# Three of four late modulation rows: from matrix-vector products on TensorE to sums on VectorE and DMA transposes

## The chip, the core and the metric

The kernel runs on one core of one Trainium2 chip. The metric is the device time of one launch in microseconds (us), the median of ten runs. The engines of a core have names used throughout: PE is TensorE (matrix products; PEld its weight loads), DVE is VectorE, ACT is ScalarE, POOL is GpSimd, and SP is the engine that here only issues DMA transfers. Each runs its own instructions in the order in which the program lists them, and waits on semaphores for the others.

## What is computed

In short form below: a transformer block with adaptive LayerNorm: a linear-attention part A and a gated feed-forward part B, both modulated by six vectors that come from a condition `c` of 1024 numbers. Sequence length S is 2048, width D 1024, feed-forward width F 3584, 32 heads of 32; inputs and output are bfloat16.

```python
mod = (silu(c) @ w_mod).reshape(c.shape[0], 6, 1, -1)
sa, ca, ga, sb, cb, gb = (mod[:, i] for i in range(6))
h = layernorm(x) * (1 + ca) + sa
q, k, v = split(h @ wqkv)
num, den = phi(q) @ (phi(k).T @ v), phi(q) @ sum(phi(k))
x = x + ga * ((num / (den + 1e-6)) @ wo)
h = layernorm(x) * (1 + cb) + sb
x = x + gb * ((silu(h @ w_gate) * (h @ w_up)) @ w_down)
```

The six vectors are six rows of 1024 numbers: each is `silu(c)` (1024) times a 1024 x 1024 block of `w_mod`. `sa` and `ca` are needed first of all. The other four, `ga`, `sb`, `cb` and `gb`, are the "late" rows. `sb` and `cb` are applied to activations whose features lie on the partitions, so they are wanted as a [128, 8] tile (feature 128 c + p at partition p, column c). `ga` and `gb` scale columns, so they are wanted spread to all 128 partitions, as the [128, 1024] tiles `ga_bc` and `gb_bc`.

## The kernel before

The 2048 positions are handled in four chunks (`sc` 0 to 3) of four tiles of 128. Groups of work on TensorE have labels, and a list written out by hand gives their order:

- V, Q and K groups: ("K", sc, i), ("V", sc, i) with i from 0 to 7, and ("Q", sc, qc). A group is eight matrix products into one PSUM bank. The order is V of chunk 0, then Q of chunk 0, K and V of chunk 1, K and V of chunk 2, K and V of chunk 3, then Q of chunks 1, 2 and 3. ("KV", sc, 0) and ("KV", sc, 1), 16 small products each into banks 5 to 7, stand before and after the first group that follows chunk sc. The text calls a label K2,3 for short, and V2 the stage of eight V groups of chunk 2.
- ("GU", sc, f) with f from 0 to 27: one gate and one up product of the feed-forward part; ("D", st, h): the down products.

`put(label, ...)` hangs further work behind a group: it is issued, on whatever engine, after that group's own instructions, and in the order in which it was put. Since every engine is in order, a label is a place in the queue of each engine that the work uses, SP's DMA queue among them.

Around the change there is this work. `phi_to` (lines 235 to 239) empties each K and Q bank: an exponential on ACT, two instructions on DVE; V banks are emptied by ACT alone. Groups take their banks in turn from five. `ln` (line 216) does the LayerNorm of one tile of the next chunk: statistics on DVE, then a power, a product and the normalisation on POOL (lines 202 to 211), then a DMA transpose on SP (line 220). It hangs behind K1,1, K1,3, K1,5 and K1,7, and the same in K2. `modulate` (line 222, two halves behind V1,4 and V1,6, and in V2) applies `sa` and `ca` on DVE to the transposed tiles, and the K groups of the next chunk read the result, one of eight slices per product. `kvz_build` (line 278) makes `KVZ` behind KV3,1; `nd_mm` (line 428) multiplies by it from Q1,3 on and normalises on DVE; `o_mm` (line 455) multiplies by `wo`.

The late rows before the change: `load_late` (line 290) brings half a row, a 1 MB block [128, 8, 512], in one of three slots `wml`; eight of them are issued from V0,6 to K2,6. `late_mm` (line 295), behind K1,2, K1,6, V1,2, V1,6, K2,2, K2,6, V2,2 and V2,6, does 32 matrix-vector products (weights 128x128, one column of `scT`) for half a row; DVE copies the finished row from PSUM to `m1`. `late_fin` makes `sbT` and `cb1T` from it, or for `ga` and `gb` a copy `rep` that repeats each column 128 times. `late_bc` (line 314, behind V1,1 and K3,1) multiplies `rep` by the identity into two banks, and ACT copies them to `ga_bc` or `gb_bc`. `wo` is loaded behind K2,0, and each of its eight slices is multiplied by `ga_bc` on DVE behind V3,0 to V3,7 (line 602). `warm` (line 185) issues products with zeros at the start.

The memory is laid out by hand: `view` cuts tiles from big regions (`M3`, `M5` and others), and tiles that live at different times share addresses.

Of the kernel before, what the change touches and what calls it, by code (L numbers as in the profile page):

```python
# [9 lines left out]
ALU = mybir.AluOpType  # L10
BF16 = mybir.dt.bfloat16
F32 = mybir.dt.float32
# [9 lines left out]
def kernel(  # L22
# [13 lines left out]
    nc = tc.nc  # L36
    P = nc.NUM_PARTITIONS
    _, S, D = A_x.shape
# [3 lines left out]
    DC = D // P  # L42
# [5 lines left out]
    NB = 512  # L48
    NH = D // NB
# [13 lines left out]
    wo_v = A_wo.rearrange("(c p) n -> p c n", p=P)  # L63
# [3 lines left out]
    wm_v = w_mod.rearrange("(p j) n -> p j n", j=DC)  # L67
    c_v = c.rearrange("o (p j) -> p (o j)", j=DC)

    const = ctx.enter_context(tc.tile_pool(name="const", bufs=1))  # L70
    dram = ctx.enter_context(tc.tile_pool(name="dram", bufs=1, space=DRAM))
    psum = ctx.enter_context(tc.tile_pool(name="psum", bufs=1, space=PSUM))
    small = ctx.enter_context(tc.tile_pool(name="small", bufs=6))
    epool = ctx.enter_context(tc.tile_pool(name="epool", bufs=4))

    x1_dram = dram.tile([S, D], F32, name="x1_scratch")
    bank = [psum.tile([P, NB], F32, name=f"bank{i}") for i in range(8)]

# [8 lines left out]
    def view(region, off, shape, dtype=BF16):  # L87
        n = 1
        for s_ in shape:
            n *= s_  # L90
        w = n * (2 if dtype == F32 else 1)
        ap = region[:, off:off + w]
        if dtype == F32:
            ap = ap.bitcast(F32)
        if len(shape) == 2:
            ap = ap.rearrange("p (a b) -> p a b", a=shape[0])
        elif len(shape) == 3:
            ap = ap.rearrange("p (a b c) -> p a b c", a=shape[0], b=shape[1])
        return ap
# [8 lines left out]
    wml = [view(M3, 4096 * (1 + i), [DC, NB]) for i in range(3)]  # L108
# [9 lines left out]
    wo = view(M6, 0, [DC, D])  # L118
    x1rs = [view(M6, 2048 * i, [D], F32) for i in range(2)]
    obs = [view(M6, 4096 + 1024 * i, [D]) for i in range(2)]  # L120
    yts = [view(M6, 6144 + 1024 * i, [NB], F32) for i in range(2)]
    xs = [view(M7, 1024 * i, [D]) for i in range(6)]
    xns = [view(M7, 6144 + 1024 * i, [D]) for i in range(6)]
    wgs = [view(M7, 4096 * i, [DC, FBW]) for i in range(3)]
# [11 lines left out]
    def load_x(st):  # L136
        nc.sync.dma_start(out=xs[st % 6], in_=x2[st * P:(st + 1) * P, :])
# [22 lines left out]
    load_wk(6, 7)  # L160
    load_wk(7, 8)

    zt = const.tile([P, NB], BF16, name="zt")
    nc.vector.memset(zt[:], 0.0)
# [15 lines left out]
    rep = const.tile([P, DC, P], BF16, name="rep")  # L180

    scT = const.tile([P, DC], BF16, name="scT")
    nc.scalar.activation(out=scT[:], in_=c_sb[:], func=ACT.Silu)

    def warm(n):
        for _ in range(n):
            nc.tensor.matmul(bank[7][:], lhsT=zt[:, 0:P], rhs=zt[:], start=True, stop=True)


    stat = {}  # L190
# [39 lines left out]
    def nextbank():  # L230
        b = bank[state["b"]]
        state["b"] = (state["b"] + 1) % 5
        return b
# [51 lines left out]
                                    in1=mask[:, P:KVW].unsqueeze(1).to_broadcast([P, n, HPC]), op=ALU.mult)  # L285


    LATE = [(2, "ga"), (3, "sb"), (4, "cb"), (5, "gb")]

    def load_late(i):  # L290
        q, kb = LATE[i // 2][0], i % 2
        k0 = q * D + kb * NB
        nc.sync.dma_start(out=wml[i % 3], in_=wm_v[:, :, k0:k0 + NB])

    def late_mm(i):
        q, kb = LATE[i // 2][0], i % 2
        mps = bank[7][:, 320 + 8 * q:328 + 8 * q]
        for ii in range(NB // P):
            col = kb * (NB // P) + ii
            for j in range(DC):  # L300
                nc.tensor.matmul(mps[:, col:col + 1], lhsT=wml[i % 3][:, j, ii * P:(ii + 1) * P],  # L301
                                 rhs=scT[:, j:j + 1], start=False, stop=(j == DC - 1), skip_group_check=True)
        if kb == 1:
            nc.vector.tensor_copy(out=m1[:, q, :], in_=mps[:, 0:DC])

    def late_fin(q):
        if q == 3:
            nc.vector.tensor_copy(out=sbT[:], in_=m1[:, 3, :])
        elif q == 4:
            nc.vector.tensor_scalar_add(out=cb1T[:], in0=m1[:, 4, :], scalar1=1.0)  # L310
        else:
            nc.vector.tensor_copy(out=rep[:], in_=m1[:, q, :].unsqueeze(2).to_broadcast([P, DC, P]))

    def late_bc(q, dst):
        for h in range(NH):
            b = nextbank()
            for i in range(NB // P):
                cc = h * (NB // P) + i
                nc.tensor.matmul(b[:, i * P:(i + 1) * P], lhsT=rep[:, cc, :], rhs=ident[:], start=True, stop=True)
            nc.scalar.copy(out=dst[:, h * NB:(h + 1) * NB], in_=b[:])  # L320


    def tr0(st):
# [40 lines left out]
    ln_xn(0, False)  # L364
    tr0(0)
    warm(3)
    ln_xn(1, False)
    tr0(1)
# [56 lines left out]
    def put(label, *fns):  # L425
        after.setdefault(label, []).extend(fns)
# [157 lines left out]
    put(("V", 0, 6), lambda: load_late(0), lambda: load_late(1), lambda: load_late(2))  # L584
# [12 lines left out]
    put(("K", 2, 0), lambda: nc.sync.dma_start(out=wo, in_=wo_v))  # L597
    put(("K", 2, 7), lambda: late_fin(4))
    put(("V", 2, 7), lambda: late_fin(5))
    put(("K", 3, 1), lambda: late_bc(5, gb_bc))  # L600
    for cc in range(DC):
        put(("V", 3, cc), lambda cc=cc: nc.vector.tensor_tensor(out=wo[:, cc, :], in0=wo[:, cc, :], in1=ga_bc[:],
                                                               op=ALU.mult))


    put(("KV", 3, 1), kvz_build)
# [77 lines left out]
```

## Time and profile before

| | us |
|---|---|
| median of ten runs | 847.27 |
| lowest, highest | 847.04, 849.18 |
| the profiled execution, its own time | 847.66 |
| its span, first to last instruction | 845.9 |

The profile is of one execution. Its times are counted from the span's start; what lies around the span is 847.66 - 845.9 = 1.8 us. Its granted TensorE clock was 1.00. A line of a timeline has the start, the length (both us), the engine, the line of the source, the instruction, output<-input with shapes, the count of instructions merged in it, and in brackets how long the engine had been idle and what ended that. A row of a group table ends with total busy us, mean ns of one, and the idle time before. A row of DMA issues ends with the median us from issue to landing.

The stages lie like this in the span (us):

| stage | from | to |
|---|---|---|
| K1 | 61.1 | 76.5 |
| V1 | 76.5 | 93.6 |
| K2, with both KV1 | 93.6 | 110.8 |
| V2 | 110.8 | 126.2 |
| K3, with both KV2 | 126.2 | 142.3 |
| V3 | 142.3 | 156.1 |
| Q1 to Q3, with `nd_mm` and `o_mm` | 156.1 | 216.4 |
| GU of chunk 0 | 216.4 | 327 |

### The profile page before, as it was taken

To read this page: it belongs to the slowest core of one execution; us is meant where nothing else is said; L and a number is where in the kernel's file an instruction comes from. 1 tells how busy PE (TensorE), PEld (TensorE's weight loads), DVE (VectorE), ACT (ScalarE), POOL (GpSimd) and SP (SyncE) were. 2 spreads that over 40 slices of the span, in tenths; PEclk is the share of its full clock that TensorE was granted. 3 is DMA by queue.
4 is the path that set the end of the run, shared out by engine and by line. 5 is a ranking of instruction groups with operands and counts; after the bars stand their busy time and mean duration, and the time that the engine had idled before them with its cause. 6 is when DMAs were issued, how large, how long until landed. Compare 5 with 4: busy or idle time off the path is not lost.

```text
span 845.9 us, 10977 instructions
## 1 busy us (share of the span) xinstructions
PE 837.5 (99%) x4452; PEld 395.5 (47%) x4452; DVE 322.9 (38%) x617; ACT 144.8 (17%) x270; POOL 78.9 (9%) x142
## 2 busy tenths in 40 slices
PE   8999999999999999999999999999999999999998
PEld 4454554544444444444444444444444444444444
DVE  5667456488755655421111222211122122112222
ACT  4333223322211111111110001111000111100000
POOL 2124130013122323100000000000000000000000
PEclk9999999999999999999999999999999999999999
DMA  9995982056489988878876215555322555201220
GB/s 292 305 239 133 276 196 54 1 126 159 96 222 216 216 215 212 195 230 255 245 232 178 69 60 163 150 150 149 106 75 70 152 156 156 84 19 62 76 69 26
DMA packets 203763, 128.65 MB, mean 152 GB/s; under 512 B 50496, under 2 KB 189888, under 8 KB 203712
## 3 DMA queue, kind: packets, MB, share of 16 engines
q1 hardware_dynamic: 162864, 98.58, 41.0%
q10 hardware_dynamic: 38544, 20.98, 11.7%
q0 software_dynamic: 2304, 8.39, 2.6%
q8 instruction: 35, 0.57, 0.3%
q14 instruction: 16, 0.13, 0.1%
HBM read 103.81 MB, written 12.58 MB: 138 GB/s over the span
## 4 chain that ended last, share of the span: by engine, by line
PE 96%; DVE 1%; SPq 1%; DMA 1%; issue 0%; ACT 0%; DVEq 0%
PE bank L530 23%; PE bank L511 23%; PE bank L505 23%; PE bank L462 7%; PE bank L265 7%; PE bank L257 6%; PE bank L242 5%; DMA M<-in_w_mod_dram 1%; PE bank L435 1%; PE bank L274 1%; PE bank L301 1%; SPq L145 1%; SPq L142 0%; DVE stats L196 0%; DVE M L239 0%; DVE e L238 0%
## 5 line engine op out<-in xcount | busy, mean ns | idle before, releaser
L511 PE MATMUL bank<-M,M 128*128 128x512 bf16 x896 | 211.7, 379 | 0.0
L505 PE MATMUL bank<-M,M 128*128 128x512 bf16 x896 | 211.6, 379 | 0.0
L513 DVE TENSOR_TENSOR M<-bank,e 128x512 bf16<-128x512 f32 x112 | 77.5, 692 | 275.1 <-PE bank L511 274.0
L530 PE MATMUL bank<-M,M 128*128 128x512 bf16 (+1 forms) x700 | 147.9, 370 | 0.0
L508 ACT ACTIVATE e<-bank 128x512 f32<-128x512 f32 x112 | 66.8, 597 | 439.7 <-PE bank L505 433.4
L530 PEld LDWEIGHTS <-M 128*128 128x128 bf16 x924 | 90.4, 98 | 103.3
L511 PEld LDWEIGHTS <-M 128*128 128x128 bf16 x896 | 87.7, 98 | 105.7
L505 PEld LDWEIGHTS <-M 128*128 128x128 bf16 x896 | 87.3, 98 | 103.9
L534 DVE TENSOR_TENSOR M<-bank,gb_bc 128x512 f32<-128x512 f32 (+1 forms) x33 | 22.3, 676 | 149.2 <-PE bank L530 149.2
L242 PE MATMUL bank<-M,M 128*128 128x512 bf16 x256 | 58.2, 379 | 1.0 <-DVE M L224 0.6
L462 PE MATMUL bank<-M,M 128*128 128x512 bf16 x256 | 57.9, 379 | 0.0
L265 PE MATMUL bank<-M,M 128*128 128x512 bf16 x256 | 57.5, 379 | 0.0
L257 PE MATMUL bank<-M,M 128*128 128x512 bf16 x256 | 56.7, 379 | 0.0
L237 ACT ACTIVATE e<-bank 128x512 f32<-128x512 f32 x64 | 37.8, 598 | 101.9 <-PE bank L265 48.4
L530 PE MATMUL bank<-M 128*128 128x512 bf16 x224 | 51.0, 379 | 0.0
L239 DVE SCALAR_TENSOR_TENSOR M<-bank,e 128x512 bf16<-128x512 f32 x64 | 44.3, 691 | 3.7
L238 DVE TENSOR_SCALAR e<-e 128x512 f32<-128x512 f32 x64 | 27.7, 433 | 40.6 <-ACT e L237 40.5
L462 PEld LDWEIGHTS <-M 128*128 128x128 bf16 x256 | 24.9, 98 | 29.8
L257 PEld LDWEIGHTS <-M 128*128 128x128 bf16 x256 | 24.7, 98 | 29.1
L265 PEld LDWEIGHTS <-M 128*128 128x128 bf16 x256 | 24.6, 98 | 27.9
L242 PEld LDWEIGHTS <-M 128*128 128x128 bf16 x256 | 24.0, 97 | 28.8 <-DVE M L224 2.1
L464 DVE TENSOR_TENSOR M<-bank,M 128x512 f32<-128x512 f32 x32 | 22.1, 690 | 14.5 <-PE bank L462 14.3
(66 smaller groups left out, 333.9 us busy)
## 6 DMA issues: line engine op xcount, KB each, us to landing
M<-in_B_w_gate_dram SPq DMA_DIRECT2D x56, 512.0 KB, 3.9
M<-in_B_w_up_dram SPq DMA_DIRECT2D x56, 512.0 KB, 5.1
M<-in_w_mod_dram SPq DMA_DIRECT2D x8, 1024.0 KB, 7.4
x_scratch<-M POOLq DMA_DIRECT2D x16, 512.0 KB, 5.7
M<-x_scratch ACTq DMA_DIRECT2D x16, 512.0 KB, 3.5
M<-in_B_w_down_dram SPq DMA_DIRECT2D x6, 1024.0 KB, 8.0
M<-in_A_x_dram SPq DMA_DIRECT2D x16, 256.0 KB, 6.7
M<-in_w_mod_dram SPq DMA_DIRECT2D x8, 512.0 KB, 8.2
```

The costliest lines, as they stand in the source:

```text
L237: nc.scalar.activation(out=e[:], in_=acc, func=ACT.Exp)
L238: nc.vector.tensor_scalar(out=e[:], in0=e[:], scalar1=1.0, scalar2=PHI_EPS, op0=ALU.min, op1=ALU.add)
L239: nc.vector.scalar_tensor_tensor(out=dst, in0=acc, scalar=0.0, in1=e[:], op0=ALU.max, op1=ALU.add)
L242: nc.tensor.matmul(acc[:], lhsT=M4[:, sc_, cc, t * P:(t + 1) * P], rhs=wk[:, cc, h * NB:(h + 1) * NB], start=(cc == 0), stop=(cc == DC - 1))
L257: nc.tensor.matmul(acc[:], lhsT=M4[:, sc_, cc, t * P:(t + 1) * P], rhs=wv[:, cc, h * NB:(h + 1) * NB], start=(cc == 0), stop=(cc == DC - 1))
L265: nc.tensor.matmul(acc[:], lhsT=wq[:, cc, qc * P:(qc + 1) * P], rhs=M4[:, sc_, cc, :], start=(cc == 0), stop=(cc == DC - 1))
L462: nc.tensor.matmul(acc[:], lhsT=oTs[st % 3][:, cc, :], rhs=wo[:, cc, hs], start=(cc == 0), stop=(cc == DC - 1))
L505: nc.tensor.matmul(g_ps[:], lhsT=wg_blk[:, cc, fs], rhs=M4[:, sc_, cc, :], start=(cc == 0), stop=(cc == DC - 1))
L508: nc.scalar.activation(out=sg[:], in_=g_ps[:], func=ACT.Silu)
L511: nc.tensor.matmul(u_ps[:], lhsT=wu_blk[:, cc, fs], rhs=M4[:, sc_, cc, :], start=(cc == 0), stop=(cc == DC - 1))
L513: nc.vector.tensor_tensor(out=gus[sc_][:, f, :], in0=u_ps[:], in1=sg[:], op=ALU.mult)
L530: nc.tensor.matmul(y_ps[:, 0:w], lhsT=gus[sc_][:, f, t * P:(t + 1) * P], rhs=wd(f)[:, c0:c1], start=(f == 0), stop=(f == FC - 1))
```

## The change

`ga`, `sb` and `gb` are no longer computed by matrix-vector products. For half a row, `late_sum` multiplies each of the eight [128, 512] slices of the weight block by a per-partition number (`scF`, `silu(c)` in float32) and adds them up in a float32 tile, eight instructions on DVE, two behind each of four labels. `late_split` writes the sum as two bfloat16 parts side by side (the rounded value and the rest). A DMA transpose on SP turns this [128, 1024] tile, so that the 128 partial sums of a feature lie along the free dimension. `late_red` sums over them on DVE and adds the two parts.

`cb` stays on the matrix-vector products (`late_vec`), in the place that `ga` had, K1,2 and K1,6. `late_bc` now writes the row from `m1` to DRAM by a DMA on POOL and reads it back, spread to 128 partitions, by a second one.

The order changes too. GA is summed in V1 and V2, SB in V3, GB in GU1,0 to GU1,8; `wo` is loaded behind K2,3 instead of K2,0, and its products with `ga_bc` stand behind K3,4 to K3,7 and V3,0 to V3,3. The two blocks of GB are loaded behind GU0,20. Four of the 24 warm-up products go, `zt` moves into `M5`, and `rep` is no longer there.

```diff
+    row_dram = [dram.tile([1, D], BF16, name=f"row_scratch{i}") for i in range(2)]
...
+    accA = view(M5, 8256, [D], F32)
+    hlA = [view(M5, 10304 + 1024 * i, [D]) for i in range(2)]
+    hltA = view(M5, 12352, [DC, P])
+    accG = view(M3, 12288, [D], F32)
+    hlG = view(M3, 14336, [D])
+    hltG = view(M3, 15360, [DC, P])
...
-    zt = const.tile([P, NB], BF16, name="zt")
+    zt = view(M5, 13376, [NB])
...
+    nc.scalar.copy(out=scF[:], in_=scT[:])
...
+    def late_sum(acc, kb, slot, js):
+        dst = acc[:, kb * NB:(kb + 1) * NB]
+        for j in js:
+            if j == 0:
+                nc.vector.tensor_scalar_mul(out=dst, in0=wml[slot][:, 0, :], scalar1=scF[:, 0:1])
+            else:
+                nc.vector.scalar_tensor_tensor(out=dst, in0=wml[slot][:, j, :], scalar=scF[:, j:j + 1], in1=dst,
+                                         op0=ALU.mult, op1=ALU.add)
+
+    def late_split(acc, kb, hl):
+        src = acc[:, kb * NB:(kb + 1) * NB]
+        nc.vector.tensor_copy(out=hl[:, 0:NB], in_=src)
+        nc.vector.tensor_tensor(out=hl[:, NB:D], in0=src, in1=hl[:, 0:NB], op=ALU.subtract)
+
+    def late_red(q, kb, hl, hlt):
+        rs = small.tile([P, DC], F32, name="rs")
+        nc.vector.tensor_reduce(out=rs[:], in_=hlt, op=ALU.add, axis=mybir.AxisListType.X)
+        cs = slice(kb * (DC // 2), (kb + 1) * (DC // 2))
+        nc.vector.tensor_tensor(out=m1[:, q, cs], in0=rs[:, 0:DC // 2], in1=rs[:, DC // 2:DC], op=ALU.add)
...
-    def late_bc(q, dst):
-        for h in range(NH):
-            b = nextbank()
-            for i in range(NB // P):
-                cc = h * (NB // P) + i
-                nc.tensor.matmul(b[:, i * P:(i + 1) * P], lhsT=rep[:, cc, :], rhs=ident[:], start=True, stop=True)
-            nc.scalar.copy(out=dst[:, h * NB:(h + 1) * NB], in_=b[:])
+    def late_bc(q, i, dst):
+        nc.gpsimd.dma_start(out=row_dram[i][0].rearrange("(c p) -> p c", p=P), in_=m1[:, q, :])
+        nc.gpsimd.dma_start(out=dst[:], in_=row_dram[i][0].partition_broadcast(P))
...
-    warm(21)
+    warm(17)
...
-    lab = [(k, sc, i) for sc in (1, 2) for k in ("K", "V") for i in (2, 6)]
-    for i in range(8):
-        put(lab[i], lambda i=i: late_mm(i))
-        if i + 3 < 8:
-            put(lab[i], lambda i=i: load_late(i + 3))
-    put(("K", 1, 7), lambda: late_fin(2))
-    put(("V", 1, 1), lambda: late_bc(2, ga_bc))
-    put(("V", 1, 7), lambda: late_fin(3))
-    put(("K", 2, 0), lambda: nc.sync.dma_start(out=wo, in_=wo_v))
-    put(("K", 2, 7), lambda: late_fin(4))
-    put(("V", 2, 7), lambda: late_fin(5))
-    put(("K", 3, 1), lambda: late_bc(5, gb_bc))
+    def sums(acc, kb, slot, labels):
+        for i, lab in enumerate(labels):
+            put(lab, lambda i=i: late_sum(acc, kb, slot, (2 * i, 2 * i + 1)))
+
+    put(("V", 0, 6), lambda: load_late(CB, 0, 0), lambda: load_late(CB, 1, 1), lambda: load_late(GA, 0, 2))
+    put(("K", 1, 2), lambda: late_vec(CB, 0, 0), lambda: load_late(GA, 1, 0))
+    put(("K", 1, 6), lambda: late_vec(CB, 1, 1), lambda: load_late(SB, 0, 1))
+    put(("V", 1, 7), lambda: late_fin())
+    def tr(hl, hlt):
+        nc.sync.dma_start_transpose(out=hlt, in_=hl)
+
+    sums(accA, 0, 2, [("V", 1, k) for k in range(4)])
+    put(("V", 1, 3), lambda: late_split(accA, 0, hlA[0]), lambda: load_late(SB, 1, 2), lambda: tr(hlA[0], hltA))
+    put(("V", 1, 7), lambda: late_red(GA, 0, hlA[0], hltA))
+    put(("K", 2, 3), lambda: nc.sync.dma_start(out=wo, in_=wo_v))
+    sums(accA, 1, 0, [("V", 2, k) for k in range(4)])
+    put(("V", 2, 3), lambda: late_split(accA, 1, hlA[1]), lambda: tr(hlA[1], hltA))
+    put(("V", 2, 7), lambda: late_red(GA, 1, hlA[1], hltA), lambda: late_bc(GA, 0, ga_bc))
     for cc in range(DC):
-        put(("V", 3, cc), lambda cc=cc: nc.vector.tensor_tensor(out=wo[:, cc, :], in0=wo[:, cc, :], in1=ga_bc[:],
-                                                               op=ALU.mult))
+        put(("K", 3, 4 + cc) if cc < 4 else ("V", 3, cc - 4),
+            lambda cc=cc: nc.vector.tensor_tensor(out=wo[:, cc, :], in0=wo[:, cc, :], in1=ga_bc[:], op=ALU.mult))
+    for kb in range(2):
+        sums(accA, kb, 1 + kb, [("V", 3, 4 * kb + k) for k in range(4)])
+    put(("V", 3, 4), lambda: late_split(accA, 0, hlA[0]), lambda: tr(hlA[0], hltA))
+    put(("KV", 3, 0), lambda: late_split(accA, 1, hlA[1]))
+    put(("Q", 1, 0), lambda: late_red(SB, 0, hlA[0], hltA), lambda: tr(hlA[1], hltA))
+    put(("Q", 1, 4), lambda: late_red(SB, 1, hlA[1], hltA), lambda: nc.vector.tensor_copy(out=sbT[:], in_=m1[:, SB, :]))
+    put(("GU", 0, 20), lambda: load_late(GB, 0, 0), lambda: load_late(GB, 1, 1))
+    for kb in range(2):
+        sums(accG, kb, kb, [("GU", 1, 5 * kb + i) for i in range(4)])
+        put(("GU", 1, 5 * kb + 4), lambda kb=kb: late_split(accG, kb, hlG), lambda: tr(hlG, hltG))
+        put(("GU", 1, 5 * kb + 6), lambda kb=kb: late_red(GB, kb, hlG, hltG))
+    put(("GU", 1, 11), lambda: late_bc(GB, 1, gb_bc))
```

More of the change, by code (lines that the diff above doesn't have):

```diff
@@ L161 @@
     load_wk(7, 8)
-    zt = const.tile([P, NB], BF16, name="zt")
-    nc.vector.memset(zt[:], 0.0)
+    zt = view(M5, 13376, [NB])
+    nc.vector.memset(zt, 0.0)
     ident = const.tile([P, P], BF16, name="ident")
@@ L179 @@
     KVZ = const.tile([P, HG, KVW], BF16, name="KVZ")
-    rep = const.tile([P, DC, P], BF16, name="rep")
+    scF = const.tile([P, DC], F32, name="scF")
     scT = const.tile([P, DC], BF16, name="scT")
     nc.scalar.activation(out=scT[:], in_=c_sb[:], func=ACT.Silu)
+    nc.scalar.copy(out=scF[:], in_=scT[:])
     def warm(n):
         for _ in range(n):
-            nc.tensor.matmul(bank[7][:], lhsT=zt[:, 0:P], rhs=zt[:], start=True, stop=True)
+            nc.tensor.matmul(bank[7][:], lhsT=zt[:, 0:P], rhs=zt, start=True, stop=True)
     stat = {}
@@ L285, in kvz_build, with load_late @@
                                     in1=mask[:, P:KVW].unsqueeze(1).to_broadcast([P, n, HPC]), op=ALU.mult)
-    LATE = [(2, "ga"), (3, "sb"), (4, "cb"), (5, "gb")]
-    def load_late(i):
-        q, kb = LATE[i // 2][0], i % 2
+    GA, SB, CB, GB = 2, 3, 4, 5
+    def load_late(q, kb, slot):
         k0 = q * D + kb * NB
[L293 to L297, printed above, removed]
+        nc.sync.dma_start(out=wml[slot], in_=wm_v[:, :, k0:k0 + NB])
@@ L298, in late_mm, with late_vec @@
+    def late_red(q, kb, hl, hlt):
[3 more added lines that the diff above has]
+        nc.vector.tensor_tensor(out=m1[:, q, cs], in0=rs[:, 0:DC // 2], in1=rs[:, DC // 2:DC], op=ALU.add)
+    def late_vec(q, kb, slot):
+        o = 320 + 8 * q
         for ii in range(NB // P):
-            col = kb * (NB // P) + ii
+            col = o + kb * (NB // P) + ii
@@ L300, in late_mm @@
             for j in range(DC):
-                nc.tensor.matmul(mps[:, col:col + 1], lhsT=wml[i % 3][:, j, ii * P:(ii + 1) * P],
+                nc.tensor.matmul(bank[7][:, col:col + 1], lhsT=wml[slot][:, j, ii * P:(ii + 1) * P],
                                  rhs=scT[:, j:j + 1], start=False, stop=(j == DC - 1), skip_group_check=True)
[L303 to L312, printed above, removed]
@@ L314, in late_bc, with late_fin @@
-    def late_bc(q, dst):
-        for h in range(NH):
-            b = nextbank()
-            for i in range(NB // P):
-                cc = h * (NB // P) + i
-                nc.tensor.matmul(b[:, i * P:(i + 1) * P], lhsT=rep[:, cc, :], rhs=ident[:], start=True, stop=True)
-            nc.scalar.copy(out=dst[:, h * NB:(h + 1) * NB], in_=b[:])
+    def late_fin():
+        nc.vector.tensor_copy(out=m1[:, CB, :], in_=bank[7][:, 320 + 8 * CB:328 + 8 * CB])
+        nc.vector.tensor_scalar_add(out=cb1T[:], in0=m1[:, CB, :], scalar1=1.0)
@@ L583 @@
                     ("V", sc - 1, 4), ("V", sc - 1, 6)])
-    put(("V", 0, 6), lambda: load_late(0), lambda: load_late(1), lambda: load_late(2))
     put(("V", 0, 7), lambda: [load_x(st) for st in range(8, 12)])
     put(("V", 1, 7), lambda: [load_x(st) for st in range(12, 16)])
-    lab = [(k, sc, i) for sc in (1, 2) for k in ("K", "V") for i in (2, 6)]
-    for i in range(8):
-        put(lab[i], lambda i=i: late_mm(i))
-        if i + 3 < 8:
-            put(lab[i], lambda i=i: load_late(i + 3))
```

## The prediction

> **What bounds the kernel now.** I read part 1 of the page and the chain of waits first.
>
> ```profile
> PE 837.5 (99%) x4452; PEld 395.5 (47%) x4452; DVE 322.9 (38%) x617; ACT 144.8 (17%) x270; POOL 78.9 (9%) x142
> PE 96%; DVE 1%; SPq 1%; DMA 1%; issue 0%; ACT 0%; DVEq 0%
> ```
>
> TensorE sets the end, so work taken from it is gained, if nothing else then makes it wait. The timeline of TensorE (start, length, work, idle before it) gives the price of the work to be removed.
>
> ```profile
> 66.29 0.94 PE L301 MATMUL bank<-scT,M 128*128 128x1 bf16 x32
> 67.10 7.07 PE L242 MATMUL bank<-M,M 128*128 128x512 bf16 x32
> 76.53 3.62 PE L257 MATMUL bank<-M,M 128*128 128x512 bf16 x16
> 81.13 0.62 PE L319 MATMUL bank<-ident,rep 128*128 128x128 bf16 x8 [0.99 <-DVE rep L312]
> 81.59 1.89 PE L257 MATMUL bank<-M,M 128*128 128x512 bf16 x8
> ...
> 131.46 0.61 PE L319 MATMUL bank<-ident,rep 128*128 128x128 bf16 x8
> 131.91 10.52 PE L242 MATMUL bank<-M,M 128*128 128x512 bf16 x48
> ```
>
> From start to start, 32 matrix-vector products take 67.10 - 66.29 = 0.81 us (the printed 0.94 has a pipeline tail), and a group of eight 512-wide products 7.07 / 4, about 1.73. The first broadcast costs 1.6: its two groups before it end at 76.53 + 3.45 = 79.98, the next starts at 81.59. The second costs 0.45.
>
> Next the timeline of VectorE, which is to take the work.
>
> ```profile
> 80.39 0.68 DVE L312 COPY rep<-m 128x1024 bf16<-128x1024 bf16 x1
> 89.95 2.67 DVE L224 TENSOR_SCALAR M<-M,ca1T,saT 128x512 bf16<-128x512 bf16 x8 [8.88 <-DMA M<-M]
> ...
> 97.01 0.43 DVE L238 TENSOR_SCALAR e<-e 128x512 f32<-128x512 f32 x1 [4.11 <-ACT e L237]
> ...
> 120.34 2.67 DVE L224 TENSOR_SCALAR M<-M,ca1T,saT 128x512 bf16<-128x512 bf16 x8 [5.53 <-DMA M<-M]
> ...
> 144.17 4.89 DVE L602 TENSOR_TENSOR M<-M,ga_bc 128x1024 bf16<-128x1024 bf16 x8
> 159.54 0.43 DVE L238 TENSOR_SCALAR e<-e 128x512 f32<-128x512 f32 x1 [10.48 <-ACT e L237]
> ...
> 175.10 1.35 DVE L444 TENSOR_TENSOR M<-bank,rd 128x384 bf16<-128x384 f32 x3
> ```
>
> Its holes lie in the V stages: 8.9 + 4.1 us in V1, 5.5 in V2, 10.5 in V3. In Q1 it has none. There two `phi_to` (2.2 us) and one normalisation (1.7) fill the 3.92 us that TensorE needs for two Q groups and one `nd_mm`: VectorE ends L444 at 176.4 and TensorE starts the next `nd_mm` at 176.56. So what VectorE is late by there, TensorE is late by too.
>
> Prices, from the page and the list of DMA issues:
>
> ```profile
> L535 DVE TENSOR_TENSOR M<-M 128x512 bf16<-128x512 f32 x31 | 21.4, 692 | 1.1
> x_scratch<-M POOLq DMA_DIRECT2D x16, 512.0 KB, 5.7
> M<-x_scratch ACTq DMA_DIRECT2D x16, 512.0 KB, 3.5
> M<-M SPq DMA_TRANSPOSE x12, 3.2
> ```
>
> **What the Trainium skill says.** "TensorE: Matmul & The Clock Gate", Back-to-back issue gap: a narrow matmul cannot start less than about 25 ns after the last. The trace agrees: 0.81 us / 32 = 25 ns; matrix-vector products are cheap already. "VectorE: DVE Perf Modes", The perf-mode tier table: float32 with two inputs, and `tensor_reduce`, run at one element per cycle. The 692 ns of L535 agree for the first; no reduce is in the trace. "SBUF — State Buffer", Who interferes with whom: a VectorE instruction with two SBUF inputs blocks a GpSimd one that reads SBUF. The trace has only a relative: the `pow` at L202 took 0.92 instead of 0.57 us beside the copy at L312. "DMA: Bandwidth & Descriptors", Rules for kernel authors: a transfer whose last dimension isn't contiguous becomes one descriptor per element. No transfer here shows that.
>
> **The change part by part.** *TensorE.* Six of eight blocks go, 6 x 0.81 = 4.9 us, and both broadcasts, 1.6 + 0.45. Sum: 6.9 us, the most that can be had: 3.2 in V1, 1.6 each in K2 and V2, 0.45 in K3.
>
> *VectorE, per half row.* A sum is a scaling (0.43, as L238) and seven `scalar_tensor_tensor`. Each reads what the last wrote; such a pair (L464, L465) starts 0.72 us apart. So 0.46 + 7 x 0.72 = 5.5. The split is 0.46 + 0.72 = 1.2. The reduce over 1024 elements I estimate at 1.2 (1024 cycles at L535's rate, (692 - 425) ns per 256 elements, is 1.07; with an overhead of 0 to 0.3), its small addition at 0.16: 1.4 in all. Sum 8.1 per half, 48 us over six; two `rep` copies of 0.69 and three casts go.
>
> *V1.* VectorE is free at 80.3 (one cast earlier than before), sums until 85.8, splits until 87.0. The last LayerNorm transpose landed at 89.9 before. GpSimd, which prepares it from 80.5 to 83.1, now works beside sums: nothing to 2.5 us later. But the weight load issued at 84.5, which shared the queue with it, now goes out at 85.9. I take 89.5, so `modulate` ends at 92.2. TensorE reaches K2,0 at 94.5 - 3.2 = 91.3 and its eighth slice at 92.8: hidden by 0.6. The GA transpose is queued behind the 1 MB load (3 to 4 us); I take a landing at 94.2 and the reduce done at 95.6. Behind it waits the first `phi_to` of K2 (ready at 93.8), 1.8 late; five banks hide that from TensorE.
>
> *K2, V2.* From 95.6 VectorE is behind: eight `phi_to` at 1.08 and four statistics at 1.69 take it to 111.1, sum and split to 117.8. The last transpose goes out near 116 and lands at 119.5; `wo`, 2 MB, is now issued in K2,3, ahead of the last two transposes, and takes 6 to 8 us from about 109. `modulate` ends at 122.2. TensorE, 6.4 us ahead of before, starts K3,0 at 127.1 - 6.4 = 120.7 and needs the eighth slice at 122.2: hidden, with nothing to spare. The reduce ends at 123.6.
>
> *The round trip of GA.* Two GpSimd DMAs, the second waiting for the first. Nearest rows: 5.7 us for a store, 3.5 for a load, both of 512 KB. The store has 2 KB but 1024 elements of two bytes, 64 per DMA engine: 3.5 us (little data) to 13 (0.15 us each, and descriptors). The load, 256 KB, 3 to 6. I take 5.4 + 4 = 9.4: `ga_bc` at 133.0. Bounds: 6.5 to 19 us.
>
> *K3, V3, Q1.* VectorE reaches the first `wo` product, queued after K3,4, at 132.2 and waits 0.8 (removing that wait would bring no more). Behind it stand the `phi_to` of K3,5 to K3,7. From 133.0: products and `phi_to` to 138.7, four products and the first sum to 146.7, second sum and splits to 154.5, `phi_to` of Q1,0 and reduce to 157.0, `kvz_build` (1.57) to 158.6. TensorE is ready for the first `nd_mm` at 158.0, 0.6 before. Then VectorE sets the pace: three `phi_to` and a normalisation to 163.6, `phi_to` of Q1,4 with the second SB reduce and `sbT` to 166.2, then two rounds to 172.9, where `nd_mm(3)` starts. It was 176.56: **3.6 us are left of the 6.9**.
>
> *Afterwards.* The 2 MB of GB at GU0,20 go ahead of weight blocks that have two blocks (21 us) to spare. In GU1 a step is 3.46 us and VectorE has 0.69 + 1.44 in it. The second SB transpose holds SP until about 160; the weight blocks behind it are needed at 216. GB's store has some 17 steps. If any of this cover fails, a wait of one to three us. The four warm-up products lay beside LayerNorm: the second transpose waits at 9.1 for ScalarE either way. Nothing, too, for `scF` (ScalarE idle until 6.3) and `zt`.
>
> The profiled execution is 847.66 (span 845.9), 0.4 above the median, so 844.1 for it and **about 843.8** against the median 847.27.
>
> **Rivals.** (a) *VectorE is not the bound*: sums run denser than 0.72 (0.61 is seen between independent instructions) and the round trip takes 7 us. Seven times 0.11 for each of the four halves up to Q1, about 3 us, comes back: 840.8. For it: those 0.61. Against: the sums are a dependent chain. (b) *Slips use up the gain*: GpSimd blocked beside the sums, or a transpose held between two 1 MB loads (one took 6.7 us against 3.2) in V1 or V2, 1.5 us each; all of it passes through `ga_bc` to Q1. 3.6 - 3 leaves 846.7. (c) *Slower: the round trip of GA.* Each us after 133.0 is a us in Q1. It breaks even at 136.6, 13 us after the reduce; by 138.3, 14.7 us, the kernel is 0.2% slower; with 17 us, `ga_bc` at 140.6, it is 7.6 - 3.6 = 4.0 us slower than before: 851.3, the middle of the case. For it: 1024 single elements and two completions in series. Against: only 2 KB, with the queues nearly idle then. (d) That VectorE does not do the sums in its holes: V3's hole of 10.5 us is too short for 13.4, which the forecast has in it.
>
> **Numbers.** Forecast 0.40, (a) 0.14, (b) 0.16, (c) 0.30. The forecast's own range is 842 to 845.5. From (a) to the middle of (c): 840.8 to 851. What a measurement can tell is 0.2%, 1.7 us: below 845.6 are forecast and (a), nearly all, 0.52; (b) is most of no change, 0.17; slower 0.31.
>
> **What would show it.** L301 with 64 pairs; the sums at 0.69 each, their starts 0.72 apart; waits of VectorE before `late_red` in V1 of two to three us and before the first `wo` product of about one; `nd_mm` waiting for `KVZ` and for the normalisations; no wait in GU. The forecast is wrong if the first `wo` product waits over four us (c), if K2,0 or K3,0 waits for `modulate` by more than one (b), or if `nd_mm` waits for nothing (a).

## The result and the profile after

| | before | after |
|---|---|---|
| median, us | 847.26 | 861.49 |
| lowest to highest | 847.04 to 849.24 | 856.68 to 862.87 |
| ratio after / before (95% interval) | | 1.0156 (1.0144 to 1.0167) |
| profiled execution, its span | 847.66, 845.9 | 862.36, 860.1 |

The kernel became slower by 1.6%, where the forecast had 843.8 and a range that ended at 851.0. The page's first part and the shares of its chain, after:

```profile
PE 837.7 (97%) x4240; PEld 390.8 (45%) x4240; DVE 369.0 (43%) x684; ACT 143.7 (17%) x267; POOL 82.7 (10%) x146
...
PE 76%; DMA 3%; DVE 0%; issue 0%; DVEq 0%
```

212 matrix instructions are gone and PE is busy for as long as before (837.5): some of its products must run slower. Its share of the span fell from 99 to 97%: it waits. And the chain, once 96% PE and 1% DMA, now goes 3% through DMA (its shares add up to 79% only, because here it could be followed back no further than to 175 us). The list of PE's waits (awaited, total us, times, longest us) has three entries of more than two us, and the kernel before has none over 1.2:

```profile
PE bank L266 <- DVE M L248: 6.5, 1, 6.5
PE bank L522 <- DMA M<-in_B_w_gate_dram: 4.4, 1, 4.4
PE bank L452 <- DVE KVZ L293: 2.6, 2, 2.4
```

Two marks of the span cut the loss in two:

```profile
182.91 1.03 PE L452 MATMUL bank<-KVZ,M 128*128 128x132 bf16 x8
...
223.17 1.89 PE L522 MATMUL bank<-M,M 128*128 128x512 bf16 x8
```

`nd_mm(3)` starts at 182.91 (before 176.56), the first gate product of the feed-forward part at 223.17 (216.42). So 6.75 us are lost by then, of the 14.2 between the spans; the other 7.45 are lost in the feed-forward part.

**The first loss: the round trip of GA.** The timeline of POOL after (start, length, queue of the instruction, and in brackets the idle time before it and its end):

```profile
123.60 1.11 POOL L336 DMA_DIRECT2D row_scratch<-m  x1 [9.35 <-DVE m L321]
139.02 0.58 POOL L337 DMA_DIRECT2D ga_bc<-row_scratch  x1 [14.31 <-DMA row_scratch<-m]
```

and of the DMA issues of the same kernel (KB each, median us from issue to landing):

```profile
ga_bc<-row_scratch POOLq DMA_DIRECT2D x1, 256.0 KB, 4.2
...
row_scratch<-m POOLq DMA_DIRECT2D x2, 2.0 KB, 18.4
```

`late_red` ends at 123.3 and the store of 2 KB is issued at 123.60, but the load behind it only at 139.02: 15.4 us for two kilobytes. (The 18.4 is the median of the two stores; the windows give 15.1 for GA's and 21.7 for GB's.) The load lands 4.2 us later, at 143.2, and VectorE has stood still for it:

```profile
143.29 0.69 DVE L625 TENSOR_TENSOR M<-M,ga_bc 128x1024 bf16<-128x1024 bf16 x1 [11.34 <-DMA ga_bc<-row_scratch]
143.90 0.42 DVE L247 TENSOR_SCALAR e<-e 128x512 f32<-128x512 f32 x1
144.42 0.69 DVE L248 SCALAR_TENSOR_TENSOR M<-bank,e 128x512 bf16<-128x512 f32 x1
```

Behind the waiting `wo` product stands the `phi_to` of K3,5 (L247, L248), with a K bank that PE wants again. PE's timeline over the same stretch:

```profile
135.08 3.62 PE L266 MATMUL bank<-M,M 128*128 128x512 bf16 x16
145.17 11.88 PE L266 MATMUL bank<-M,M 128*128 128x512 bf16 x48 [6.47 <-DVE M L248]
156.88 1.07 PE L283 MATMUL bank<-M 128*128 128x129 bf16 x16
```

PE stops for 6.47 us, and then needs 11.7 us from start to start for six groups that are 6 x 1.73 = 10.4 us elsewhere. In Q1 it waits once more, 2.37 us, because `kvz_build` stands in VectorE's queue behind all that is late there; the two Q groups that start at 169.25 then take 4.74 us instead of 3.46. Why the products after a wait are slow, the view by windows says (length, then busy us and count of PE, PEld, DVE, ACT and POOL, then granted clock, DMA share, GB/s):

```profile
142.00:144.00 2.00, 0.00 (x0) 0.00 (x0) 0.71 (x2) 0.00 (x0) 0.00 (x0) 0.50 0.25 57
169.00:171.00 2.00, 2.00 (x9) 0.82 (x7) 1.93 (x5) 0.54 (x2) 0.00 (x0) 0.50 0.68 133
432.00:434.00 2.00, 1.78 (x5) 0.69 (x6) 0.00 (x0) 0.00 (x0) 0.10 (x1) 0.50 0.92 330
```

The granted clock is 0.50 at the end of each of the three waits or right after it. "TensorE: Matmul & The Clock Gate", Part 1, in the Trainium skill says that an idle time of about 3.4 us sets the array back to half its clock. For the first and the last wait the trace agrees, so such a wait costs more than its length. But it is no safe lower bound: the clock also fell after the wait of only 2.37 us for `KVZ`. In the trace it fell 2.4, 2.7 and 3.4 us after PE had stopped, and stayed at half for 6.8, 3.4 and 6.8 us.

**The second loss: the store of GB.** It is issued at 409.53 and lands 21.7 us later, and nothing waits for `gb_bc` for a long time. But the view of DMAs from 409 to 432 us (first row: GB/s in 40 equal slices) reads after:

```profile
GB/s 292 364 356 319 304 293 290 265 230 234 39 3 0 0 0 29 38 21 19 13 6 19 20 24 45 56 80 94 53 21 35 43 86 75 77 49 44 29 124 271
...
M<-in_B_w_gate_dram SPq DMA_DIRECT2D x2, 512.0 KB, 20.0
M<-in_B_w_up_dram SPq DMA_DIRECT2D x2, 512.0 KB, 14.7
...
row_scratch<-m POOLq DMA_DIRECT2D x1, 2.0 KB, 21.7
```

and the same stretch before:

```profile
GB/s 111 221 327 345 302 335 392 330 227 256 292 280 244 283 290 249 191 274 338 370 367 306 329 334 279 282 285 205 87 19 0 10 152 246 345 216 130 252 302 315
...
M<-in_B_w_gate_dram SPq DMA_DIRECT2D x3, 512.0 KB, 5.4
M<-in_B_w_up_dram SPq DMA_DIRECT2D x3, 512.0 KB, 5.2
```

From the eleventh slice (414.8 us) until shortly before the store has landed, the core moves less than 100 GB/s. Weight blocks on another queue, SP's, land after 20.0 and 14.7 us (medians of two each) instead of 5.4 and 5.2. SP's timeline shows that it is held up already in issuing:

```profile
419.22 12.12 SPq L510 DMA_DIRECT2D M<-in_B_w_gate_dram  x1
```

The issue of a gate block takes 0.37 us in the median of its 56, and this one 12.12. In the kernels below it is the same wherever a store of elements side by side stands next to these loads (longest issue 12.35 with GA mended, 11.04 with the `wo` products later, 13.50 in the first look at prices), and where none does, no issue of a gate block in this stretch takes over 1 us. What holds SP there is not shown. So PE runs out of weights in spite of the two blocks in stock:

```profile
432.22 3.60 PE L522 MATMUL bank<-M,M 128*128 128x512 bf16 x8 [4.39 <-DMA M<-in_B_w_gate_dram]
435.60 3.12 PE L528 MATMUL bank<-M,M 128*128 128x512 bf16 x8
438.56 1.89 PE L522 MATMUL bank<-M,M 128*128 128x512 bf16 x8
```

4.39 us of waiting, then 3.38 and 2.96 us (from start to start) at half clock for two groups of 1.73: 4.39 + 2.88 = 7.3 of the 7.45.

### The profile page after: what moved, and what is told of

The parts are those of the page before. It is cut to its first block, busy times and chain, and to the rows that moved or that the text cites. A ratio compares the mean times of both kernels' runs of the same rounds, so it can differ in the third digit from the quotient of the medians.

```text
span 860.1 us, 10627 instructions
## 1 busy us (share of the span) xinstructions
PE 837.7 (97%) x4240; PEld 390.8 (45%) x4240; DVE 369.0 (43%) x684; ACT 143.7 (17%) x267; POOL 82.7 (10%) x146
## 4 chain that ended last, share of the span: by engine, by line
PE 76%; DMA 3%; DVE 0%; issue 0%; DVEq 0%
PE bank L547 22%; PE bank L522 22%; PE bank L528 22%; PE bank L479 6%; PE bank L274 3%; DMA M<-in_B_w_gate_dram 2%; DMA M<-M 1%; PE bank L452 1%; DVE M L461 0%; DVE M L551 0%; DVE M L552 0%; DVEq L461 0%
## 5 line engine op out<-in xcount | busy, mean ns | idle before, releaser
L248 DVE SCALAR_TENSOR_TENSOR M<-bank,e 128x512 bf16<-128x512 f32 x64 | 44.2, 691 | 3.9
L247 DVE TENSOR_SCALAR e<-e 128x512 f32<-128x512 f32 x64 | 27.7, 433 | 16.0 <-ACT e L246 16.0
L481 DVE TENSOR_TENSOR M<-bank,M 128x512 f32<-128x512 f32 x32 | 22.0, 688 | 14.2 <-PE bank L479 14.1
```

The lines of the kernel that those rows point to most:

```text
L247: nc.vector.tensor_scalar(out=e[:], in0=e[:], scalar1=1.0, scalar2=PHI_EPS, op0=ALU.min, op1=ALU.add)
L248: nc.vector.scalar_tensor_tensor(out=dst, in0=acc, scalar=0.0, in1=e[:], op0=ALU.max, op1=ALU.add)
```

## The experiments

The theory after this reading (A): both losses come from the two stores of a row to DRAM, each element by itself, and all else of the change does what it should. The rivals: (B) VectorE's added load is the loss, and the stores only show it; (C) the two GpSimd DMAs in series are slow by themselves, whatever is stored. Later a question within A: what makes the store slow. The kernel before, measured beside each of these kernels, had medians of 847.2 to 847.4.

**GA without the round trip.** The row is spread by products of a repeated copy with the identity, as it was before; GB keeps its round trip.

```diff
-    put(("V", 2, 7), lambda: late_red(GA, 1, hlA[1], hltA), lambda: late_bc(GA, 0, ga_bc))
+    put(("V", 2, 7), lambda: late_red(GA, 1, hlA[1], hltA), lambda: late_rep(GA))
+    put(("K", 3, 2), lambda: late_bc_pe(ga_bc))
```

> The changed kernel with ga alone spread by TensorE again (rep copy behind V2,7, sixteen small products behind K3,2); gb still goes through DRAM. Theory A, the element-wise store of ga is what holds VectorE 11.3 us before the first wo product: that wait is gone, nd_mm(3) starts near 173 us as the prediction's walk had it, not at 183, and about 10 us come back: 851 to 852. Theory B, VectorE's new work itself is the load: the wait only moves, at most 3 us come back: 858 or more.

Measured: 848.3 (846.05 to 851.54), ratio 1.0005 (0.9991 to 1.0019). In its timelines the first `wo` product and `nd_mm(3)`:

```profile
131.87 0.68 DVE L638 TENSOR_TENSOR M<-M,ga_bc 128x1024 bf16<-128x1024 bf16 x1
...
171.47 0.73 PE L464 MATMUL bank<-KVZ,M 128*128 128x132 bf16 x8
```

No wait in brackets before the product, and `nd_mm(3)` is 11.4 us earlier than in the changed kernel, with all the sums still on VectorE: B falls. The wait of 4.5 us for `w_gate` is still there, and GB's store landed after 21.9 us. More came back (861.49 - 848.3 = 13.2 us) than the 10 that were expected, and than the 6.75 lost by the start of the feed-forward part: the gain of the change, which the wait had used up, came back with it, and GB's loss is not the same in each run.

**GB without the round trip.** The same edit for GB, and GA as in the change.

> The changed kernel with gb alone spread by TensorE again (rep copy behind GU1,11, products behind GU1,13); ga still goes through DRAM. Theory A, the store of gb clogs the DMA engines and makes the weight loads of GU1 late: the 4.4 us wait of TensorE for w_gate and its slow clock after it are gone, about 7 us come back: 854. Theory B, the 2 MB of gb weights and the transposes on SP make them late: no more than 1 us comes back, 860.5 or more, with the wait still there.

Measured: 854.09 (852.86 to 856.03), ratio 1.0069 (1.0048 to 1.0091). The waits of this kernel:

```profile
PE bank L267 <- DVE M L249: 4.8, 1, 4.8
...
DVE M L637 <- DMA ga_bc<-row_scratch: 9.7, 1, 9.7
```

The wait in the feed-forward part is gone, the wait for `ga_bc` stays: the losses are separate, one to each store. The rival in this expectation falls too, because the 2 MB of GB's weights and the transposes on SP are all still there.

**Both stores in runs of 16 bytes.** Everything stays as in the change, also the two DMAs in series; only the order in DRAM differs, so that a partition writes its eight numbers side by side. `ga` and `gb` therefore stand in another order of columns, and the kernel leaves out putting them right, so it is of use for its time only.

```diff
-        nc.gpsimd.dma_start(out=row_dram[i][0].rearrange("(c p) -> p c", p=P), in_=m1[:, q, :])
+        nc.gpsimd.dma_start(out=row_dram[i][0].rearrange("(p c) -> p c", c=DC), in_=m1[:, q, :])
```

> The changed kernel, but the two stores write eight numbers of a partition side by side (128 runs of 16 bytes instead of 1024 single elements); ga and gb so come out in another order of columns, all else is computed as before. Theory A, single elements are the price: each store lands in 3 to 4 us instead of 15 and 22, both losses go: 843.5 to 845. Theory C, two GpSimd DMAs in series are slow whatever their shape: the wait before the first wo product stays above 5 us: 853 or more.

Measured: 843.55 (843.28 to 846.21), ratio 0.9957 (0.9945 to 0.997). POOL's timeline (this one execution took 846.21, and was behind by 1.8 us from K1 on):

```profile
126.09 0.75 POOL L336 DMA_DIRECT2D row_scratch<-m  x1 [10.11 <-DVE m L321]
128.28 0.56 POOL L337 DMA_DIRECT2D ga_bc<-row_scratch  x1 [1.44 <-DMA row_scratch<-m]
```

2.2 us from issue to issue instead of 15.4, with the same bytes on the same queue. C falls, and with one line of an access pattern the whole 18 us come back. It lands at the forecast of 843.8, which had taken 5.4 us for this store; GA's took 1.9, and GB's, beside the weight loads, 5.6.

**A first look at prices.** Six stores of different shapes added to the kernel before, behind down groups.

> The kernel before, with six stores of a [128, 8] tile to unused DRAM added one by one in the down products of chunks 2 and 3, where the DMA queues are nearly idle; 847 to 848 us. If the price is per element: 1024 elements of two bytes from GpSimd 12 to 15 us, 512 of them 7 to 9, 128 runs of 16 bytes 3, 1024 from ScalarE's queue 12 to 15, 1024 of four bytes 12 to 15. If it is GpSimd's making of descriptors, the one from ScalarE's queue takes 3 to 5. If it is neighbours in one stretch of DRAM, the 1024 elements set 512 bytes apart take 3 to 5; if not, 12 to 15.

It did not measure what it should. POOL's queue follows nothing of PE, so four of the stores were issued at 347 to 349 us, one on another, and their landings (19.6 to 25.0 us) can't be told apart; the fifth, of 4-byte elements, was issued at 375 beside the delayed weights (9.4 us). Alone was only the one on ACT's queue: 15.5 us. But the heap of four stood beside the loads of gate and up weights, and the launch, a single one, took 859.56 instead of 847.42. The timeline of PE:

```profile
375.10 3.52 PE L510 MATMUL bank<-M,M 128*128 128x512 bf16 x8 [9.05 <-DMA M<-in_B_w_gate_dram]
```

So the second loss can be put into the kernel before, where no sum, transpose or reduce of the change exists.

**The `wo` products later.** Both round trips stay; the products move behind V3,4 to V3,7, and SB's sums take their place.

```diff
-        put(("K", 3, 4 + cc) if cc < 4 else ("V", 3, cc - 4),
+        put(("V", 3, 4 + cc // 2),
...
-        sums(accA, kb, 1 + kb, [("V", 3, 4 * kb + k) for k in range(4)])
-    put(("V", 3, 4), lambda: late_split(accA, 0, hlA[0]), lambda: tr(hlA[0], hltA))
+        sums(accA, kb, 1 + kb, [("V", 3, k) if kb else ("K", 3, 4 + k) for k in range(4)])
+    put(("V", 3, 0), lambda: late_split(accA, 0, hlA[0]), lambda: tr(hlA[0], hltA))
```

> The changed kernel with both DRAM round trips as they are, but the reader of ga_bc later: the sums of sb stand behind K3,4 to V3,3, the eight wo products two each behind V3,4 to V3,7, so that VectorE has other work for the 20 us that ga_bc takes. Theory A, the round trip costs only because VectorE stands at the first wo product: no wait there, nd_mm(3) near 172 to 173 us as with ga spread by TensorE, 847.5 to 849 (what gb costs stays). Theory B, VectorE's work up to Q1 is too much whatever its order: 857 or more.

Measured: 848.91 (845.34 to 852.96), ratio 1.0021 (1.001 to 1.0032). The products start at 147.94 without a wait, `nd_mm(3)` at 172.10, and of PE's waits over 1.5 us only the one in the feed-forward part is left:

```profile
PE bank L522 <- DMA M<-in_B_w_gate_dram: 3.3, 1, 3.3
```

So the slow store of GA costs nothing where the instruction that waits for it has nothing urgent behind it; GB's, for which nothing waits, costs about as before (848.91 here, 848.3 with GA mended). They are two mechanisms: one store is late for its reader, the other keeps the other queues from their data.

**No transposes, no reduce, no DRAM.** A product with ones on TensorE adds up the partitions of the two bfloat16 parts, for `ga` and `gb` spread to all partitions in the same step.

```diff
+    def late_ones(kb, hl, dst):
+        b = nextbank()
+        for h in range(2):
+            nc.tensor.matmul(b[:], lhsT=ones[:], rhs=hl[:, h * NB:(h + 1) * NB], start=(h == 0), stop=(h == 1))
+        nc.scalar.copy(out=dst[:, kb * NB:(kb + 1) * NB], in_=b[:])
...
-    put(("V", 2, 7), lambda: late_red(GA, 1, hlA[1], hltA), lambda: late_bc(GA, 0, ga_bc))
+    put(("K", 3, 0), lambda: late_ones(1, hlA[1], ga_bc))
```

> The sums of the changed kernel on VectorE, but the sum over partitions on TensorE: for ga and gb a product of a 128x128 tile of ones with the two parts of the sum (four 512-wide products per row, ScalarE copies the bank to ga_bc or gb_bc), for sb one-column products (16 in all); no transpose of sums, no reduce, no DRAM. TensorE: 6.9 us taken off, 0.86 + 0.86 + 0.4 put back. VectorE loses four halves of waits and reduces. If TensorE is then the bound everywhere: 842.5. If VectorE still sets the pace in Q1: 844 to 845.

Measured: 843.0 (842.55 to 843.6), ratio 0.9949 (0.9931 to 0.9967); `nd_mm(3)` at 170.45, and no wait of PE over 1.2 us. The lowest median of all, between the two cases of the expectation.

**Runs of 8 bytes, in the right order.** The split writes its columns permuted, so that after the transpose a partition has four neighbouring numbers of each half, and the stores go in 256 runs of 8 bytes.

```diff
-        nc.gpsimd.dma_start(out=row_dram[i][0].rearrange("(c p) -> p c", p=P), in_=m1[:, q, :])
+        nc.gpsimd.dma_start(out=row_dram[i][0].rearrange("(k p c) -> p k c", k=2, c=4),
+                            in_=m1[:, q, :].rearrange("p (k c) -> p k c", k=2))
```

> The changed kernel with the right order of columns kept and the stores in 256 runs of 8 bytes: the split writes the columns of ga and gb in another order, so that a partition holds four neighbours of the row after the transpose. If the price is per run, a store lands in 5 to 7 us instead of 15 and 22: ga_bc some 2 us later than with 128 runs, 844 to 846. If it is the pieces under some larger size that cost, whatever their number, 850 or more.

Measured: 843.92 (843.45 to 844.54), ratio 0.9958 (0.9942 to 0.9974). GA's store landed after 3.4 us, less than the 5 to 7 expected, GB's after some 8, beside the weight loads:

```profile
124.19 0.92 POOL L339 DMA_DIRECT2D row_scratch<-m  x1 [9.93 <-DVE m L324]
127.94 0.59 POOL L341 DMA_DIRECT2D ga_bc<-row_scratch  x1 [2.83 <-DMA row_scratch<-m]
```

This is the change as it stands with its one fault mended: `nd_mm(3)` at 171.97, where the forecast had 172.9.

**Both rows by TensorE.** The edits of the first two experiments together.

> The changed kernel with ga and gb both spread by TensorE from the rep copy, as before the change, so that nothing of it goes through DRAM; sums, transposes and reduces as changed. Against 843.6 and 843.9 with the quick stores it pays 0.9 us of small products: 844 to 845. If some of what the two parts alone left (848.3 and 854.1) is not the store: 846 or more.

Measured: 843.47 (843.23 to 843.96), ratio 0.9953 (0.9936 to 0.9969). The three ways to mend it (843.0, 843.47, 843.92) differ by less than their spreads can tell; what unites them is that no store of lone elements side by side is left.

**What makes the store slow.** Two kernels, each the one before with single stores added far apart among the down groups, each tied to PE's progress by a small copy on VectorE.

```diff
+    def probe(label, src, eng, dst, n=DC):
+        put(label, lambda: nc.vector.tensor_copy(out=src, in_=m1[:, 2, :]),
+            lambda: eng.dma_start(out=dst, in_=src[:, 0:n]))
...
+    probe(("D", 4, 1), prs[2], nc.gpsimd, colv(pr[2], 2), 2)
+    probe(("D", 8, 0), prs[3], nc.gpsimd, colv(pr[3]))
+    probe(("D", 12, 1), prs[6], nc.gpsimd, wide(prw[1], 32))
```

> The kernel before, with eight stores of a [128, 8] tile to unused DRAM, each tied by a small VectorE copy to a place of its own in the down products, 12 us or more apart. Per element: 128 runs of 16 bytes 3 us, 512 single elements 8, 256 of them 5, 1024 of four bytes 12 to 15, 1024 of two bytes from GpSimd 15 and from ScalarE's queue 15. If neighbours in DRAM are what makes single elements slow, 1024 of them 512 bytes apart take 5 or less and 64 bytes apart something between; if not, 12 to 15 as well. Time 848 to 850.

> The kernel before with six more stores to unused DRAM, as in the probe before: what counts there was not the number of elements (256, 512 and 1024 single ones took 15 to 16 us) but that they are neighbours (64 bytes apart: 3.4 us). If the stores into one short stretch of DRAM are done one after the other, about 0.4 us each over 64 bytes, then two-byte elements 4 bytes apart (16 to a stretch) take 8 to 10 us, 8 bytes apart 5 to 6, 16 bytes apart 4, 32 bytes apart 3.5, and 128 elements side by side still 14 to 16; 128 runs of 32 bytes 3.5. If only elements that touch each other are slow, every spacing takes 3 to 4.

The first kernel took 848.03, the second 847.58: such stores among the down groups, one at a time, cost next to nothing. DMA issues of the first:

```profile
prA<-rep POOLq DMA_DIRECT2D x1, 2.0 KB, 3.6
prB<-rep POOLq DMA_DIRECT2D x1, 1.0 KB, 15.9
prC<-rep POOLq DMA_DIRECT2D x1, 0.5 KB, 16.3
prf<-rep POOLq DMA_DIRECT2D x1, 4.0 KB, 10.1
prE<-rep POOLq DMA_DIRECT2D x1, 2.0 KB, 14.7
prF<-rep ACTq DMA_DIRECT2D x1, 2.0 KB, 15.1
```

and of the second:

```profile
prA<-rep POOLq DMA_DIRECT2D x1, 0.2 KB, 15.6
prf<-rep POOLq DMA_DIRECT2D x1, 4.0 KB, 1.7
```

The stores of elements set apart (`prw`) stand there as medians only. One by one, from the DMA view over a short window at each (512 and 64 bytes apart in the first kernel, then 4, 8, 16 and 32 in the second):

```profile
prw<-rep POOLq DMA_DIRECT2D x1, 2.0 KB, 3.0
...
prw<-rep POOLq DMA_DIRECT2D x1, 2.0 KB, 3.8
...
prw<-rep POOLq DMA_DIRECT2D x1, 2.0 KB, 10.5
...
prw<-rep POOLq DMA_DIRECT2D x1, 2.0 KB, 5.3
...
prw<-rep POOLq DMA_DIRECT2D x1, 2.0 KB, 3.4
...
prw<-rep POOLq DMA_DIRECT2D x1, 2.0 KB, 3.2
```

In words, each in one execution (us from issue to landing):

| what is stored | 2-byte elements side by side | other |
|---|---|---|
| 128 / 256 / 512 / 1024 elements | 15.6 / 16.3 / 15.9 / 14.7 | |
| 1024 elements, ACT's queue | 15.1 | |
| 1024 elements of 4 bytes, side by side | | 10.1 |
| 1024 elements of 2 bytes, starts 4 / 8 / 16 / 32 bytes apart | | 10.5 / 5.3 / 3.4 / 3.2 |
| the same, 64 / 512 bytes apart | | 3.8 / 3.0 |
| 128 runs of 16 / 32 bytes | | 3.6 / 1.7 |

An eighth of the elements takes as long as all of them: the idea that each lone element has a price falls, which was also the prediction's, and with it the 8 and 5 us expected for 512 and 256 of them. ACT's queue takes as long as POOL's, so it is not something that GpSimd alone does in making the transfer. With 16 bytes or more from start to start the store is quick; the closer than that its elements lie, the longer it takes. Differences of under some two us say nothing: the store of 128 runs of 16 bytes took 3.6 us here, and GA's of the same shape 1.9.

Here "DMA: Bandwidth & Descriptors", Specifications, which states that transfers under 512 bytes are done as read-modify-write, is not enough: 1024 elements of two bytes are all far under it, and go from 3.0 to 14.7 us by their spacing alone. The second kernel's expectation, that elements in one short stretch of DRAM are written one after the other, came near (15.6, 10.5, 5.3, 3.4 and 3.2 measured for 14 to 16, 8 to 10, 5 to 6, 4 and 3.5; only the runs of 32 bytes were off, 1.7 for 3.5). That each must be read, changed and written back before its neighbour would fit; no run here shows it, nor why the weight loads have to wait meanwhile. Spacing is also not all: 256 runs of 8 bytes without gaps, GA's store above, landed after 3.4 us, and 1024 elements 8 bytes apart after 5.3.

## Why the prediction was wrong

Its walk along the stages up to the store was right to within two microseconds, in part because errors cancelled (the sums of V1 ended one us late, but `modulate` behind them found its transpose there and did not wait):

| step of the prediction | forecast | measured |
|---|---|---|
| sums and splits of the first half done | 87.0 | 87.97 |
| `modulate` of V1 done | 92.2 | 90.6 |
| first reduce done | 95.6 | 95.4 |
| `modulate` of V2 done | 122.2 | 121.8 |
| K3,0 starts | 120.7 | 120.36 |
| second reduce done | 123.6 | 123.3 |
| GA's store from issue to landing | 5.4 (3.5 to 13) | 15.1 |
| `ga_bc` there | 133.0 | 143.2 |
| `nd_mm(3)` starts | 172.9 | 182.91 |

- **The step that failed: "The round trip of GA".** "The store has 2 KB but 1024 elements of two bytes, 64 per DMA engine: 3.5 us (little data) to 13 (0.15 us each, and descriptors)... I take 5.4 + 4 = 9.4". Measured were 15.1 + 4.2, with a little around them: 19.9 from the reduce to `ga_bc`, above the bound of 19. The load was right. The bound was built on a price for each element, 0.15 us, for which the trace before had no line and which the experiments refute: 128 elements take 15.6 us as well. The nearest row, a store of 512 KB in long runs, was no relative of it.
- **Rival (c) named the mechanism, and its rule held.** "Each us after 133.0 is a us in Q1": `ga_bc` came 10.2 us late and `nd_mm(3)` 10.0. Its sign was there as well: the first `wo` product waited 11.34 us, where over four was to mean (c). The way there was partly another: TensorE lost 6.47 us already in V3, through the banks behind the `phi_to` of K3,5, and 1.4 at half clock, and in Q1 2.6 waiting for `KVZ`. Its own price was based on 17 us, and its chance was 0.30; had its cost been the only one, the end would have been at about 854, as the experiment with GB mended has it.
- **The second step that failed: "Afterwards".** "GB's store has some 17 steps" counted the time until its reader needs it, and that was right: nothing waits for `gb_bc`. It costs 7.45 us in the trace by what it does to other transfers. Of the weight loads the prediction asked only what stands before them in SP's queue, not what a transfer on POOL's queue takes from them. "A wait of one to three us" was foreseen if cover failed; it was 4.39 and half clock after it. No rival had it. The range was missed without it too: GA's store alone ends at 854.
- **Rival (a), VectorE not the bound, and (d), no sums in the holes**, are not what happened. The timeline of VectorE after has the sums at this pace:

```profile
80.57 6.30 DVE L309 SCALAR_TENSOR_TENSOR M<-M,scF,M 128x512 f32<-128x512 bf16 x7
...
82.15 2.36 DVE L309 SCALAR_TENSOR_TENSOR M<-M,scF,M 128x512 f32<-128x512 bf16 x2
...
93.96 1.22 DVE L319 TENSOR_REDUCE rs<-M 128x8 f32<-128x1024 bf16 x1 [3.04 <-DMA M<-M]
...
159.28 4.68 DVE L309 SCALAR_TENSOR_TENSOR M<-M,scF,M 128x512 f32<-128x512 bf16 x6
```

4.68 / 6 = 0.78 each, where the prediction took 0.72: 0.4 us too little in a half row. In GA's two halves it is 1.3: of the seven sums that start at 80.57 six go at that pace, and one of the two in the second line (the third of the seven) takes twice as long; the half in V2 is 6.30 long too. The reduce (forecast 1.2) and VectorE's wait for it (forecast two to three) fit.
- **Rival (b), slips beside GpSimd.** "SBUF — State Buffer", Who interferes with whom, has VectorE and GpSimd contend for a shared pair of ports, as an exclusive lock, when a VectorE instruction with two inputs in SBUF meets a GpSimd one that reads it. The trace agrees in what it shows: the one long sum is the one that starts during GpSimd's normalisation (81.56 to 83.18), which itself takes 1.62 instead of 1.19. That looks like one waiting for the other; no run here separates it from a mutual slowing. It was absorbed.
- **The gain that was forecast is real.** With quick stores and little else changed, 843.55 and 843.92 stand against 843.8; 3.6 us of the 6.9 were to be left, and 847.3 - 843.9 = 3.4 are. What hid it was 10.5 us through GA's store (854.09 - 843.55: only GA's store slow, against both in runs of 16 bytes) and 4.8 through GB's (848.3 - 843.55: only GB's slow); together 858.8, and the measured 861.49 leaves 2.7 unaccounted for. In the profiled executions the half clock after GB's wait lasted 6.8 us in the changed kernel and 3.4 in the one with GA mended, which may be a part of it. GB's share varies: single runs of the kernel with GA mended lie between 846 and 851.5.

## What to carry to other kernels

Look at the spacing of what a DMA writes to DRAM, not only at its size: two kilobytes as lone 2-byte neighbours took 15 us here, and in runs of 8 bytes or more 2 to 8. A wait placed on an in-order engine costs what stands behind it, so put the first reader of a slow transfer where nothing urgent follows; and a transfer for which nobody waits must still be asked what it does to the loads on other queues while it runs. When TensorE has to wait for more than about two microseconds, look up the granted clock after the wait: here the products behind waits of 2.4 us and more ran at half clock for a while, and that belongs to the price of the wait.

## What the runs showed that was not expected

- Lone 2-byte elements side by side land after 14.7 to 16.3 us, whether 128 or 1024 of them; starts 4 bytes apart take 10.5, 8 bytes 5.3, 16 bytes and more 3.0 to 3.8.
- While such a store runs beside weight loads, the core's DMA traffic falls from some 300 to below 100 GB/s, and 512 KB loads on another queue take 20.0 and 14.7 us instead of 5.4 and 5.2. The store itself is slower there too (21.7 us), and SP takes 12.12 us to issue one block.
- TensorE's granted clock fell to 0.50 between 2.4 and 3.4 us after it had stopped, once although the wait was over after 2.37 us.
- A chained, in-place `scalar_tensor_tensor` over 512 columns goes at 0.78 us each; one of seven took twice that beside GpSimd's normalisation.
